# The 640-point transform stages of a spectral filter, from quarter folds with a remainder chunk to five 128x128 tables by residues modulo 5

## The chip, the core and the metric

The kernel runs on one core of a Trainium2 chip. The metric is the device time of one execution in microseconds (us), the median over the runs shown. TensorE multiplies, VectorE and ScalarE read the results out of PSUM and do the elementwise work, GpSimd makes tables and SyncE (SP) issues nearly all DMAs; each engine works through its own queue in the order in which the program gives it instructions.

## What is computed

The reference, cut to what matters: a layer norm, a global spectral filter over the 2048 x 640 tile, a gated feed-forward network on the same normalised input, and a sum.

```python
xn = _layernorm(x)                                  # x: 1 x 2048 x 640, bf16
X  = rfft2(xn.astype(float32))                      # over (2048, 640): 2048 x 321
s  = irfft2(X * (w_r + 1j * w_i), s=(2048, 640)).astype(bfloat16)
g  = silu((gelu(xn @ w_gate) * (xn @ w_up)) @ w_down)   # 640 -> 1536 -> 640
out = x + s * g
```

## The kernel before, in words

Row n = 16 n2 + n1 of x is partition n2 of slab n1: 16 slabs of 128 x 640. The 2048-point transform is split into 16 x 128 and the 640-point transform uses the symmetry of cosine and sine. The stages of the spectral part are, slab by slab:

- **fold** (`fold_a`, `fold_b` with `fold4`, two slabs at a time, VectorE): sums and differences of a row with its mirror image, so that a 640-long row becomes five chunks of 128 columns. Four chunks are full quarters, the fifth collects the remaining columns.
- **S1** (`slab_S1`): five matmuls of a chunk by the 128-point table `Tfwd`, 128 columns each; ScalarE casts the result to Z.
- **D** (`slab_D` with `d_matmuls`, L481 to 484): the 640-point stage. Four outputs of 161 columns, and for each one matmul by `FT` and one by the remainder table `TR`: eight matmuls of 161 columns. ScalarE casts it to `zd`, a DMA writes it to DRAM (`ZDR`).
- **load_B2**, then 16 **quads** (`quad_S2`, `quad_S2i`): the 16-point stage on 64x64 quarters of TensorE (`px`), a cast to `xs` by ScalarE, two products with the filter tables W1 and W2 on VectorE (`p1`, `p2`), the inverse 16-point stage (`pu`), a cast, and DMAs to DRAM (`UDR`).
- **load_V**, **vfold** (VectorE, as the fold), **S1i** (five matmuls of 128 columns) and **Di** (`slab_Di`, again `d_matmuls`): ScalarE scales the result to `eo`, VectorE makes the two halves of a row of Y from it by one addition and one subtraction (L587, L588).
- **finish / multiply_add** (L596 to 598): Y times the gate G plus x, and the DMA of a row to the output.

The feed-forward network is what TensorE mostly does: for each group g of four slabs twelve tiles t of the gate (`psg`) and of the up projection (`psu`), five matmuls each (L623); ScalarE makes `ge` from psg (L628), VectorE multiplies it with psu to uT (L630); then the down projection (L647), `th` (ScalarE, L677) and G (VectorE, L678). psg and psu have two PSUM banks each, all results of the spectral stages share two further buffers (`psB`).

The order is written out by hand. The list `back` holds the network in 144 **slots**: slots 0 to 13 are 256 columns of a tile (both projections), slots 14 to 23 half a tile each (512 columns of psg in even slots, of psu in odd ones), slots 24 to 35 the down projection of group 0 in thirds; then 24 half tiles and 12 thirds for each further group: 36 to 71, 72 to 107, 108 to 143. `plan[s]` lists what of the spectral part follows in slot s, and every engine gets its instructions in that order. So an instruction that waits holds up all that stand behind it on its engine. Before, S1 and D of slab 4 onward stand some three slots apart up to slot 58, the quads at 66 to 91, S1i and Di at 102 to 134. The sine tables of the second half of the 128-point table are made by ScalarE in slot 22 (`tinv_sin`, `mg_sin`; two loads of the activation table), the statistics and the norm (`stats`, `root4`, `norm`, `norm_act`) group by group ahead of the folds.

Of the kernel before, what the change touches and what calls it, by code (L numbers as in the profile page):

```python
# [14 lines left out]
P = 128  # L15
S = 2048
D = 640
# [13 lines left out]
def kernel(  # L31
# [36 lines left out]
    W1 = [wts.tile([P, 2, 8, L], BF16, name=f"W1{b}") for b in range(2)]  # L68
    W2 = [wts.tile([P, 2, 8, L], BF16, name=f"W2{b}") for b in range(2)]
# [6 lines left out]
def build(nc, env):  # L76
    consts, big, wts, xg, work, psA, psB = (env[k] for k in ("consts", "big", "wts", "xg", "work", "psA", "psB"))
# [26 lines left out]
    def w_rows(i, b, half, ri, pm):  # L104
        q0 = half * 64 + ri * 2 + pm
        return spw[i][0][b][q0:q0 + 61:4]

    def w_plus(i, b, half, ri):
        r = b * 16 + half * 8
        src = spw[i][1][:, 0:64].rearrange("k (a r) l -> k a r l", a=2)  # L110
        nc.sync.dma_start(out=w_rows(i, b, half, ri, 0), in_=src[:, :, r:r + 8, :])

    def w_minus(i, b, lo, half):
        sp = spw[i][1]
        WT = w_rows(i, b, half, 0, 1)
        r = 128 - lo * 32 - b * 16 - half * 8
        s0 = 1 if r == 128 else 0
        nc.sync.dma_start(out=WT[:, lo, s0:8, :], in_=sp[:, r - s0:r - 8:-1, :])
        if s0:
            nc.sync.dma_start(out=WT[:, lo, 0, :], in_=sp[:, 64, :])  # L120

    def w_dup(i, b, half):
        nc.sync.dma_start(out=w_rows(i, b, half, 1, 1), in_=w_rows(i, b, half, 0, 1))

    def w_edge(i, b):
        WT = spw[i][0][b].rearrange("p a s l -> p (a s) l")[:, :, 0:L:320]
        nc.gpsimd.tensor_scalar(out=WT, in0=WT, scalar1=0.5, scalar2=None, op0=ALU.mult)
# [3 lines left out]
    FT = consts.tile([P, 5, LH], BF16)  # L131
    TR = consts.tile([P, 2, 2, LH], BF16)
# [36 lines left out]
    lint = gtile([LH], INT32)  # L169
    nc.gpsimd.iota(lint, pattern=[[1, LH]], base=0, channel_multiplier=0)  # L170
    vt = gtile([NS, P], INT32)

# [21 lines left out]
    u_f, hi_f, s_f, h_f, g_f, pf, lo_b = bits("pb", [(0, 63), (6, 1), (0, 31), (5, 1), (5, 3), (0, 127), (0, 1)])  # L194
    ph_t = affine("ph_t", hi_f, -1536.0, 1536.0)
    e96 = c1("e96")
    nc.vector.tensor_single_scalar(out=e96, in_=pf, scalar=96.0, op=ALU.is_equal)
    a_m = affine("a_m", pf, 2.0, 64.0)
    b_o = affine("b_o", pf, 1.0, 32.0)
    sp_f = c1("sp_f")  # L200
    nc.vector.tensor_scalar(out=sp_f, in0=e96, scalar1=160.0, scalar2=s_f, op0=ALU.mult, op1=ALU.add)
    b_e = affine("b_e", h_f, -160.0, 160.0)
    a_r = affine("a_r", sp_f, 2.0, 0.0)
    b_r = c1("b_r")
    nc.vector.tensor_scalar(out=b_r, in0=sp_f, scalar1=hi_f, scalar2=b_e, op0=ALU.mult, op1=ALU.add)
# [39 lines left out]
    fv = gtile([3, LH], FP32)  # L245
    ftm = gtile([3, LH], FP32)

    def ft_angle():
        nc.scalar.activation(out=fv[:, 0], in_=lint, func=ACT.Identity, scale=a_m)
        nc.scalar.activation(out=fv[:, 1], in_=lint, func=ACT.Identity, scale=a_m, bias=b_o)  # L250
        nc.scalar.activation(out=fv[:, 2], in_=lint, func=ACT.Identity, scale=a_r, bias=b_r)
        nc.scalar.activation(out=ftm, in_=fv, func=ACT.Identity, scale=1.0 / 640.0, bias=magic)
        nc.scalar.activation(out=ftm, in_=ftm, func=ACT.Identity, bias=nmagic)

    def ft_wrap():
        nc.vector.scalar_tensor_tensor(out=fv, in0=ftm, scalar=-640.0, in1=fv, op0=ALU.mult, op1=ALU.add)

    def ft_sin():
        w = TWO_PI / 640.0 * (1.0 - 2e-7)
        nc.scalar.activation(out=ftm[:, 0:2], in_=fv[:, 0:2], func=ACT.Abs)  # L260
        nc.scalar.activation(out=FT[:, 1:4:2], in_=fv[:, 0:2], func=ACT.Sin, scale=w)
        nc.scalar.activation(out=FT[:, 4], in_=fv[:, 2], func=ACT.Sin, scale=w)
        nc.scalar.activation(out=FT[:, 0:4:2], in_=ftm[:, 0:2], func=ACT.Sin, scale=-w, bias=halfpi)

    def ft_rest():
        nc.gpsimd.memset(mhalf, -0.5)
        mk4 = consts.tile([P, 4], FP32)
        for g in range(4):
            nc.vector.tensor_single_scalar(out=mk4[:, g:g + 1], in_=g_f, scalar=float(g), op=ALU.is_equal)
        for g in range(4):  # L270
            nc.vector.tensor_scalar(out=TR[:, g // 2, g % 2, :], in0=FT[:, 4, :], scalar1=mk4[:, g:g + 1],
                                    scalar2=None, op0=ALU.mult)
        nc.gpsimd.memset(TR[32:33, 0, 0, 0:LH:2], 1.0)
        nc.gpsimd.memset(TR[32:33, 0, 0, 1:LH:2], -1.0)
# [144 lines left out]
    def fold4(dst, src, plus, minus):  # L419
        s4 = src.rearrange("p k (t d) -> p k t d", t=2)  # L420
        dm = dst[:, :, 0:512].rearrange("p k (g d) -> p k g d", g=4)
        dr = dst[:, :, 512:640].rearrange("p k (g d) -> p k g d", g=4)
        for gs, op in ((plus, ALU.add), (minus, ALU.subtract)):
            nc.vector.tensor_tensor(out=dm[:, :, gs, :], in0=s4[:, :, :, 32:160], in1=s4[:, :, :, 288:160:-1], op=op)
            nc.vector.tensor_tensor(out=dr[:, :, gs, 1:32], in0=s4[:, :, :, 1:32], in1=s4[:, :, :, 319:288:-1], op=op)

    def fold_a(pair):
        xn = X[:, 2 * pair:2 * pair + 2, :]
        assert ("n", 2 * pair + 1) in done
        uvt = work.tile([P, 2, D], BF16, tag="uv", bufs=1)  # L430
        nc.vector.tensor_tensor(out=uvt[:, :, 0:320], in0=xn[:, :, 0:320], in1=xn[:, :, 320:640], op=ALU.add)
        nc.vector.tensor_tensor(out=uvt[:, :, 320:640], in0=xn[:, :, 0:320], in1=xn[:, :, 320:640], op=ALU.subtract)
        xf[pair] = uvt

    def fold_b(pair):
        uvt = xf[pair]
        f = work.tile([P, 2, D], BF16, tag="xf", bufs=2)
        fold4(f, uvt, slice(0, 4, 3), slice(1, 3))
        nc.vector.tensor_copy(out=f[:, :, 512:D:32], in_=uvt[:, :, 0:D:160])
        xf[pair] = f  # L440
        done.add(("f", pair))

    def chunk(f, k, c):
        return f[:, k, c * P:(c + 1) * P]
# [25 lines left out]
    def slab_S1(n1):  # L470
# [3 lines left out]
        for c in range(5):  # L474
            nc.tensor.matmul(pz[:, c, :], lhsT=chunk(f, n1 % 2, c), rhs=Tfwd[:, n1, :], start=True, stop=True)  # L475
# [3 lines left out]
    def d_matmuls(ps, lhs):  # L479
        for b in range(2):  # L480
            for k in range(2):  # L481
                o = ps[:, b, k * LH:(k + 1) * LH]
                nc.tensor.matmul(o, lhsT=lhs[:, 2 * b + k, :], rhs=FT[:, 2 * b + k, :], start=True, stop=False)  # L483
                nc.tensor.matmul(o, lhsT=lhs[:, 4, :], rhs=TR[:, b, k, :], start=False, stop=True)  # L484

    def natural(ps):
        return ps[:, :, 0:LP].rearrange("p b (c m) -> p c m b", c=2)

    def slab_D(n1):
        pd = psB.tile([P, 2, 512], FP32, tag="b")  # L490
        d_matmuls(pd, Zt.pop(n1))
        zd = work.tile([P, 2, LP], BF16, tag="m2", bufs=3)
        nc.scalar.copy(out=zd.rearrange("p c (m b) -> p c m b", b=2), in_=natural(pd))  # L493
        nc.sync.dma_start(out=ZDR[:, n1].rearrange("c p l -> p c l"), in_=zd[:, :, 0:L])
# [12 lines left out]
    def quad_S2(j):  # L507
# [8 lines left out]
        nc.scalar.copy(out=xs, in_=px[:, :, 0:L])  # L516
        p1 = work.tile([P, 2, L], BF16, tag="p1", bufs=3)
        p2 = work.tile([P, 2, L], BF16, tag="p2", bufs=3)
        for pp, WT in ((p1, W1), (p2, W2)):
            nc.vector.tensor_tensor(out=pp, in0=xs, in1=WT[j // 8][:, :, j % 8, :], op=ALU.mult)  # L520
# [4 lines left out]
    def quad_S2i(j):  # L525
# [9 lines left out]
        us = work.tile([P, 2, L], BF16, tag="m2", bufs=3)  # L535
        nc.scalar.copy(out=us, in_=pu[:, :, 0:L])  # L536
        for lo in range(2):
            to = uv[lo][:, j // 8, :, j % 8, :]
            nc.sync.dma_start(out=to[:, :, 0:L], in_=us[lo * 64:lo * 64 + 32, :, :])
            nc.sync.dma_start(out=to[:, :, L:D], in_=us[lo * 64 + 32:lo * 64 + 64, :, 1:320])  # L540
# [12 lines left out]
    def vfold(pair):  # L553
        V = st_c["V"][:, 2 * pair:2 * pair + 2, :]
        f = work.tile([P, 2, D], BF16, tag="xf", bufs=2)
        fold4(f, V, slice(0, 4, 3), slice(2, 0, -1))
        nc.vector.tensor_tensor(out=f[:, :, 512:513], in0=V[:, :, 0:1], in1=V[:, :, 320:321], op=ALU.add)
        nc.vector.tensor_tensor(out=f[:, :, 576:577], in0=V[:, :, 0:1], in1=V[:, :, 320:321], op=ALU.subtract)
        nc.vector.tensor_copy(out=f[:, :, 544:D:64], in_=V[:, :, 160:D:320])
        st_c[("f", pair)] = f  # L560

# [157 lines left out]
    for n1 in range(4, NS):  # L719
        if n1 == 7:  # L720
            s += 2
# [138 lines left out]
```

## Time and profile before

| | |
|---|---|
| median of 3 runs | 211.51 us (211.3 to 211.68) |
| the profiled execution | 212.3 us, of which the span in the trace 210.5 us |
| busy time | TensorE 200.3 us, VectorE 138.2, ScalarE 127.7, GpSimd 19.2 |
| first and last matmul of the network | begins at 10.67 us, ends at 207.25 us |
| last instruction of VectorE | ends at 208.13 us |
| VectorE busy from 156.8 to 192.8 us | 31.31 of 36.00 us |

A row of the groups gives line, engine, operation, result and inputs, shape and count, then the busy time in us and the mean duration in ns of one, then the idle time of the engine before them and who ended it. In the timeline the first number is the start, the second the duration; independent instructions of one engine overlap a little, so the distance from start to start is below the duration. The chain of work is the path followed back from the last instruction; in order of time its rows give start, length and what ran.

### The profile page before, as it was taken

The page shows a single profiled execution, that of the slowest core. Times are in us where ns is not written, and L with a number is a line of the kernel's source. Part 1 is how long each engine was busy: PE and PEld are TensorE (multiplying, and loading weights), DVE is VectorE, ACT ScalarE, POOL GpSimd, SP SyncE. Part 2 cuts the span into 40 slices and gives each one's busy share as a digit, 9 for nine tenths or more (in the row PEclk, how much of TensorE's full clock was granted, in tenths as well). Part 3 has the DMA queues.
Part 4 walks back from the last instruction along what each step waited for, and adds up shares of the span by engine and source line. Part 5 has one row for each costly group of instructions (what it writes and reads, how often), then busy time and mean ns, then how long its engine had stood idle before and what let it go on. Part 6 is the DMA issues. An engine that isn't in the chain of part 4 may idle for free.

```text
span 210.5 us, 4486 instructions
## 1 busy us (share of the span) xinstructions
PE 200.3 (95%) x1600; PEld 125.5 (60%) x1600; DVE 138.2 (66%) x436; ACT 127.7 (61%) x215; POOL 19.2 (9%) x53
## 2 busy tenths in 40 slices
PE   0699999999999999999999999999999999999993
PEld 0389984567765555666644434347776556666773
DVE  8878977975975662252566755423769888994443
ACT  7656567599575666532677767732466665665721
POOL 8000128720004000000000000000000000000000
PEclk9999999999999999999999999999999999999999
DMA  5999955765946575739963232328913443332221
GB/s 159 337 361 366 361 159 137 159 165 147 175 78 164 134 175 124 195 120 205 221 131 82 64 86 67 88 68 247 340 42 96 121 120 101 97 93 65 63 78 47
DMA packets 37222, 31.79 MB, mean 151 GB/s; under 512 B 11344, under 2 KB 35024, under 8 KB 37072
## 3 DMA queue, kind: packets, MB, share of 16 engines
q1 hardware_dynamic: 37200, 31.51, 55.5%
q8 instruction: 12, 0.20, 0.4%
q14 instruction: 10, 0.08, 0.1%
HBM read 20.34 MB, written 7.87 MB: 134 GB/s over the span
## 4 chain that ended last, share of the span: by engine, by line
PE 95%; DVE 3%; ACT 1%; issue 0%; POOL 0%; POOLq 0%
PE psg L623 25%; PE psu L623 25%; PE psg L647 13%; PE psu L647 12%; PE pu L533 2%; PE pz L475 2%; PE py L484 2%; PE pd L484 2%; PE pd L483 2%; PE py L483 2%; PE pv L572 2%; PE px L513 2%; PE pw L279 1%; DVE st L371 1%; ACT Tinv L219 1%; PE pt L453 1%
## 5 line engine op out<-in xcount | busy, mean ns | idle before, releaser
L623 PE MATMUL psg<-xnT,Wg 128*128 128x512 bf16 (+1 forms) x275 | 61.5, 355 | 0.0
L623 PE MATMUL psu<-xnT,Wu 128*128 128x512 bf16 (+1 forms) x275 | 61.2, 354 | 0.0
L630 DVE TENSOR_TENSOR uT<-psu,ge 128x512 bf16<-128x512 f32 (+1 forms) x55 | 34.0, 618 | 26.3 <-PE psu L623 25.0
L647 PEld LDWEIGHTS <-uT 128*128 128x128 bf16 x396 | 37.2, 98 | 14.3 <-issue 0.5
L628 ACT ACTIVATE ge<-psg 128x512 bf16<-128x512 f32 (+1 forms) x55 | 30.0, 546 | 20.4 <-PE psg L623 18.9
L623 PEld LDWEIGHTS <-Wg 128*128 128x128 bf16 x275 | 25.6, 99 | 20.0 <-issue 2.3
L623 PEld LDWEIGHTS <-Wu 128*128 128x128 bf16 x275 | 25.6, 99 | 19.7 <-issue 1.8
L647 PE MATMUL psg<-Wd,uT 128*128 128x320 bf16 (+1 forms) x204 | 31.1, 295 | 0.0
L647 PE MATMUL psu<-Wd,uT 128*128 128x320 bf16 (+1 forms) x192 | 28.9, 295 | 0.0
L520 DVE TENSOR_TENSOR p<-xs,W 128x642 bf16<-128x642 bf16 x32 | 14.5, 493 | 9.7 <-ACT xs L516 9.4
L584 ACT ACTIVATE eo<-py 128x644 bf16<-128x644 f32 x16 | 11.3, 707 | 9.8 <-PE py L484 9.6
L516 ACT CAST xs<-px 128x642 bf16<-128x642 f32 x16 | 11.1, 694 | 9.2 <-PE px L513 5.8
L493 ACT CAST zd<-pd 128x644 bf16<-128x644 f32 x16 | 11.1, 694 | 6.0 <-PE pd L484 6.0
L371 DVE BATCH_NORM_STATS2 st<-X 128x6 f32<-128x320 bf16 x32 | 13.9, 477 | 0.0
L596 DVE TENSOR_TENSOR Yall<-Yall,G 128x640 bf16<-128x640 bf16 (+2 forms) x21 | 8.7, 412 | 7.7 <-ACT G L683 7.3
L477 ACT CAST Z<-pz 128x640 bf16<-128x640 f32 x16 | 11.0, 688 | 4.0 <-PE pz L475 4.0
L574 ACT CAST vs<-pv 128x640 bf16<-128x640 f32 x16 | 11.0, 688 | 2.0 <-PE pv L572 2.0
L536 ACT CAST us<-pu 128x642 bf16<-128x642 f32 x16 | 11.2, 700 | 0.9 <-PE pu L533 0.9
L678 DVE SCALAR_TENSOR_TENSOR G<-th,psg 128x320 bf16<-128x320 f32 x12 | 5.8, 482 | 8.8 <-ACT th L677 8.7
L677 ACT ACTIVATE th<-psu 128x320 f32<-128x320 f32 x12 | 5.3, 439 | 8.6 <-PE psu L647 8.5
L483 PE MATMUL py<-FT,vs 128*128 128x161 bf16 x64 | 10.5, 233 | 0.0
L483 PE MATMUL pd<-FT,Z 128*128 128x161 bf16 x64 | 10.5, 233 | 0.0
(140 smaller groups left out, 235.8 us busy)
## 6 DMA issues: line engine op xcount, KB each, us to landing
ZDR<-zd SPq DMA_DIRECT2D x16, 160.5 KB, 3.0
B<-ZDR SPq DMA_DIRECT2D x8, 321.0 KB, 7.2
xt<-in_A_x_dram SPq DMA_DIRECT2D x16, 160.0 KB, 2.4
Wg<-in_B_w_gate_dram SPq DMA_DIRECT2D x4, 480.0 KB, 7.4
Wu<-in_B_w_up_dram SPq DMA_DIRECT2D x4, 480.0 KB, 8.4
X<-in_A_x_dram SPq DMA_DIRECT2D x3, 640.0 KB, 9.1
Wd<-in_B_w_down_dram SPq DMA_DIRECT2D x1, 1920.0 KB, 13.9
Vin<-UDR SPq DMA_DIRECT2D x3, 640.0 KB, 7.6
```

What stands on the lines that cost most here:

```text
L371: nc.vector.bn_stats(out=st[:, k, :], in_=xr[:, k, :])
L477: nc.scalar.copy(out=Zt[n1], in_=pz)
L483: nc.tensor.matmul(o, lhsT=lhs[:, 2 * b + k, :], rhs=FT[:, 2 * b + k, :], start=True, stop=False)
L493: nc.scalar.copy(out=zd.rearrange("p c (m b) -> p c m b", b=2), in_=natural(pd))
L516: nc.scalar.copy(out=xs, in_=px[:, :, 0:L])
L520: nc.vector.tensor_tensor(out=pp, in0=xs, in1=WT[j // 8][:, :, j % 8, :], op=ALU.mult)
L536: nc.scalar.copy(out=us, in_=pu[:, :, 0:L])
L584: nc.scalar.activation(out=eo.rearrange("p c (m b) -> p c m b", b=2), in_=natural(py), func=ACT.Copy, scale=(2.0 if n1 >= 12 else 1.0) / ( ...
L623: nc.tensor.matmul(ps, lhsT=WT[:, c, t * P:(t + 1) * P], rhs=xnT[g][:, c, c0:c1_], start=(c == 0), stop=(c == 4))
L628: late.append(lambda: nc.scalar.activation(out=ge, in_=ps, func=ACT.Gelu_apprx_tanh))
L630: nc.vector.tensor_tensor(out=uT[g][:, t, c0:c1_], in0=ps, in1=cur["ge"], op=ALU.mult)
L647: nc.tensor.matmul(ph, lhsT=uT[g][:, t, j * P:(j + 1) * P], rhs=Wd[:, t, c0:c1_], start=(t == 0), stop=(t == NT - 1))
```

## The change

- **Fold.** `fold_a` adds and subtracts a slab and its mirror image in pieces of 64 columns to T (two additions of 640 columns per pair of slabs). `fold_b` makes two differences of 512 columns and two scaled additions (`scalar_tensor_tensor`, 512 columns each, factors 0.618 and -1.618), `fold_c` three additions of 512, 256 and 256. They stand in three slots of their own for each pair.
- **D** is five matmuls of 128 columns by blocks of a new table FT (640 columns); TR and its making go. `zd` is written into one of three buffers `ZB`.
- **Di** is five matmuls of 128 columns by FI, five transposes of FT (`fi_turn`, slot 61). **vfold goes**: the inverse quads write their rows to DRAM in the order that S1i needs, with two casts on ScalarE and one on VectorE (256 columns each) in place of one of 642 on ScalarE. In its place stand `spread_a` and `spread_b` after Di, per pair of slabs: two scaled additions, four additions of 512 columns and two of 640; L587 and L588 go.
- `multiply_add` of slabs 0 to 11 stands at slots written out (109 to 139) and no longer where its inputs are ready; the rows of x that it adds are loaded into W1 once the filter is used up.
- **Filter loads**: one tile each for W1 and W2, 28 DMAs in place of 48, in slots 14 to 47; edges in slot 55.
- **Order.** The pairs' folds, S1 and D stand at slots written out, the second sine tables are made in slot 26 in place of 22, the statistics, roots and norms are moved, D ends in slot 56, quads stand at 65 to 89 with the inverse part ahead of the forward one, S1i and Di at 98 to 130.

The core of the diff (after.py against before.py):

```diff
-    def fold_b(pair):
-        uvt = xf[pair]
-        f = work.tile([P, 2, D], BF16, tag="xf", bufs=2)
-        fold4(f, uvt, slice(0, 4, 3), slice(1, 3))
-        nc.vector.tensor_copy(out=f[:, :, 512:D:32], in_=uvt[:, :, 0:D:160])
+    def fold_b(pair):
+        W = xf[pair].rearrange("p a k (m d) -> p (a k) m d", d=64)
+        NM = work.tile([P, 2, 4, 2, 64], BF16, tag="nm", bufs=1, name="NM")
+        nm = NM.rearrange("p i q x d -> p q i x d")
+        for x, i0, i1 in ((0, slice(4, 2, -1), slice(1, 3)), (1, slice(0, 2), slice(3, 1, -1))):
+            nc.vector.tensor_tensor(out=nm[:, :, :, x, :], in0=W[:, :, i0, :], in1=W[:, :, i1, :], op=ALU.subtract)
+        f = work.tile([P, 5, 2, P], BF16, tag="xf", bufs=2, name="f")
+        fc = f[:, 1:5].rearrange("p (a c) k d -> p c a (k d)", c=2)
+        for c, g in ((0, TAU), (1, -NU)):
+            nc.vector.scalar_tensor_tensor(out=fc[:, c], in0=NM[:, 1].rearrange("p (a k) x d -> p a (k x d)", a=2), scalar=g,
+                                           in1=NM[:, 0].rearrange("p (a k) x d -> p a (k x d)", a=2),
+                                           op0=ALU.mult, op1=ALU.add)
+    def fold_c(pair):
+        T, f = xf[pair]
+        W = T.rearrange("p a k (m d) -> p (a k) m d", d=64)
+        pq = work.tile([P, 4, 2, 64], BF16, tag="pq", bufs=1, name="pq")
+        nc.vector.tensor_tensor(out=pq, in0=W[:, :, 1:3, :], in1=W[:, :, 4:2:-1, :], op=ALU.add)
+        nc.vector.tensor_tensor(out=pq[:, :, 0, :], in0=pq[:, :, 0, :], in1=pq[:, :, 1, :], op=ALU.add)
+        nc.vector.tensor_tensor(out=f[:, 0].rearrange("p k (a d) -> p a k d", a=2),
+                                in0=pq[:, :, 0, :].rearrange("p (a k) d -> p a k d", a=2),
+                                in1=T[:, :, :, 0:64], op=ALU.add)
...
     def slab_D(n1):
-        d_matmuls(pd, Zt.pop(n1))
+        for c in range(5):
+            nc.tensor.matmul(pair_of(cols, *FWD[c]), lhsT=Z[:, c, :], rhs=block2(FTf, c), start=True, stop=True)
...
+        us = ZB[j % 3].rearrange("p (h r q) -> p h r q", h=2, r=6)
+        nc.scalar.copy(out=us[:, :, 1:4:2, :], in_=residues(pu, 1, 1))
+        nc.scalar.copy(out=us[:, :, 2:5:2, :], in_=residues(pu, 4, -1))
+        nc.vector.tensor_copy(out=us[:, :, 0:6:5, :], in_=residues(pu, 0, 5))
...
+    def spread_a(pair):
+        nc.vector.scalar_tensor_tensor(out=NM[:, 0].rearrange("p q x d -> p q (x d)"), in0=H, scalar=TAU, in1=G,
+                                       op0=ALU.mult, op1=ALU.add)
+        nc.vector.scalar_tensor_tensor(out=NM[:, 1].rearrange("p q x d -> p q (x d)"), in0=G, scalar=TAU, in1=H,
+                                       op0=ALU.mult, op1=ALU.subtract)
+        nc.vector.tensor_tensor(out=Eb[:, :, 4:2:-1, :], in0=a2, in1=nm[:, :, :, 0, :], op=ALU.add)
+        nc.vector.tensor_tensor(out=Eb[:, :, 1:3, :], in0=a2, in1=nm[:, :, :, 0, :], op=ALU.subtract)
+    def spread_b(pair):
+        nc.vector.tensor_tensor(out=Eb[:, :, 0:2, :], in0=Eb[:, :, 0:2, :], in1=m12, op=ALU.add)
+        nc.vector.tensor_tensor(out=Eb[:, :, 3:1:-1, :], in0=Eb[:, :, 3:1:-1, :], in1=m12, op=ALU.subtract)
+        nc.vector.tensor_tensor(out=up, in0=e4[:, 0], in1=e4[:, 1], op=ALU.add)
+        nc.vector.tensor_tensor(out=down, in0=e4[:, 0], in1=e4[:, 1], op=ALU.subtract)
...
+    fold_at = ((3, 5, 7), (8, 10, 12), (19, 20, 22), (26, 28, 30), (32, 33, 35), (38, 41, 43), (45, 46, 48), (49, 50, 52))
+    s1_at = ((9, 10, 11, 12), (14, 15, 16, 17), (23, 24, 26, 27), (31, 32, 34, 35), (36, 38, 39, 41), (44, 45, 47, 48),
+             (49, 50, 51, 52), (53, 54, 55, 56))
+    for g, st, nf in ((1, (13, 14, 15, 16), (18, 20)), (2, (23, 24, 26, 27), (31, 33)), (3, (36, 37, 39, 40), (44, 46))):
...
-    put(19, tinv_wrap, 1)
-    put(22, tinv_sin, 1)
-    put(22, mg_sin)
+    put(21, tinv_wrap, 1)
+    put(26, tinv_sin, 1)
+    put(26, mg_sin)
+    put(z_end + 1, mg_build)
+    put(z_end + 3, mg_turn)
+    put(z_end + 5, fi_turn)
...
+    for p in range(8):
+        sd = vs0 + 4 * p + 5 if p < 7 else s
+        put(sd + 1, spread_a, p)
+        put(sd + 2, spread_b, p)
+    for n1, sl in enumerate((109, 114, 119, 124, 129, 131, 133, 134, 135, 136, 138, 139)):
+        put(sl, multiply_add, n1, 0, D)
```

In `s1_at` the four numbers of a pair are the slots of S1 and S1, D and D of its two slabs; in `fold_at` the three are the slots of `fold_a`, `fold_b`, `fold_c`; z_end is 56, vs0 is 98.

## Prediction

> **What bounds it now.** I read the page's totals, the slices and the chain first.
>
> ```profile
> PE 200.3 (95%) x1600; PEld 125.5 (60%) x1600; DVE 138.2 (66%) x436; ACT 127.7 (61%) x215; POOL 19.2 (9%) x53
> ...
> DVE  8878977975975662252566755423769888994443
> ...
> PE 95%; DVE 3%; ACT 1%; issue 0%; POOL 0%; POOLq 0%
> ```
>
> TensorE is the chain; from 10.67 to 207.25 us it never waits for long. But VectorE, 66% on average, is at 7 to 9 tenths at both ends, where the folds and the inverse stage lie. So each matmul removed is worth its time only while VectorE and ScalarE keep up. The chain in order of time gives TensorE's prices:
>
> ```profile
> 6.88 1.86 PE pw L279 x4
> ...
> 70.81 0.28 PE pz L475 x5
> 71.09 1.08 PE psu L623 x5
> ...
> 72.73 1.08 PE psg L623 x5
> ```
>
> S1 (five matmuls of 128) takes 0.276, half a tile 1.08, and from 72.17 to 72.73 a D stage fits: 0.545 for eight matmuls of 161. VectorE's prices come from the groups (mean ns of one is the number behind busy) and its timeline:
>
> ```profile
> L424 DVE TENSOR_TENSOR f<-uvt 128x512 bf16<-128x512 bf16 x16 | 6.8, 424 | 0.1
> L431 DVE TENSOR_TENSOR uvt<-X 128x640 bf16<-128x640 bf16 x8 | 4.0, 494 | 4.1 <-ACT X L411 3.6
> L256 DVE SCALAR_TENSOR_TENSOR GEN<-GEN 128x483 f32<-128x483 f32 x1 | 0.7, 657 | 0.0
> ```
>
> ```profile
> 164.47 0.49 DVE L596 TENSOR_TENSOR Yall<-Yall,G 128x640 bf16<-128x640 bf16 x1
> 165.00 0.49 DVE L597 TENSOR_TENSOR Yall<-Yall,xt 128x640 bf16<-128x640 bf16 x1
> 165.41 0.68 DVE L630 TENSOR_TENSOR uT<-psu,ge 128x512 bf16<-128x512 f32 x1
> ```
>
> An instruction that needs the one before it starts 0.04 after its end (164.47 to 165.00), any other 0.08 before it (165.00 to 165.41).
>
> **TensorE.** 32 stages (16 D, 16 Di) fall from 0.545 to the 0.276 of five matmuls of 128: -8.6. The five transposes of `fi_turn` add 0.28. Together **-8.3**.
>
> **VectorE, per pair of slabs.** Additions of n bf16 columns: 0.49 for 640, 0.42 for 512, 0.29 for 256 (between the 124 and 320 column rows, 0.22 and 0.33). That 64-column runs and reversed blocks cost no more I take from L424, which reads backwards in two dimensions. A scaled addition of 512 bf16 columns isn't in the trace: from below 0.42 (the addition), from above 0.69 (L256, 483 columns in 0.657, a column per tick). I take 0.69, the same operation. [...]
>
> With the distances: fold_a 0.82; fold_b 0.34 + 0.46 + 2 x 0.61 = 2.03; fold_c 0.46 + 0.33 + 0.21 = 1.00. So 3.85 where the old fold took 1.83 (17.34 to 19.50 less a uT). Spread_a 0.61 + 0.73 + 0.34 + 0.46 = 2.15, spread_b 0.34 + 0.46 + 0.82 = 1.63: 3.78 where vfold (1.22) and four additions of L587, L588 (1.1) took 2.3. The casts of `us` add about 0.34 (256 columns out of PSUM; the 0.42 of a uT of 256) in the quads, where VectorE is at 5 to 7 tenths. VectorE's total rises by some 34 us to 172, against 192 of TensorE: no spare at the ends.
>
> **Waits ahead of S1.** TensorE takes S1 in order, so if fold_c is late everything waits. For each pair I add up both queues from a common point. In slots: uT 0.61, stats 1.04, norm 0.4, G 0.41; TensorE 1.08 per half tile, 1.09 per third, 0.276 per unit; uT starts 0.12 after its matmuls.
>
> - *Slot 23.* From the end of slot 18: VectorE stands behind the uT of slot 19 until 1.2, then uT 0.61, fold_a 0.82, fold_b 2.03, norm 0.4, uT 0.61, the wrap of the angles 0.6, fold_c 1.08: 7.35. TensorE arrives after five half tiles, 5.42. **Wait 1.9.**
> - *Slot 31.* ScalarE holds the second sine tables now in slot 26, one slot pair ahead of a fold:
>
> ```profile
> 43.01 1.28 ACT L219 ACT_TABLE_LOAD   x1
> 44.31 1.15 ACT L219 ACTIVATE Tinv<-GEN,negpi 128x1024 bf16<-128x1024 int32 x1
> ...
> 45.84 0.67 ACT L477 CAST Z<-pz 128x640 bf16<-128x640 f32 x1
> 46.53 1.28 ACT L677 ACT_TABLE_LOAD   x1
> 47.82 0.44 ACT L677 ACTIVATE th<-psg 128x320 f32<-128x320 f32 x1
> ```
>
> ```profile
> 48.29 0.49 DVE L678 SCALAR_TENSOR_TENSOR G<-th,psg 128x320 bf16<-128x320 f32 x1 [2.29 <-ACT th L677]
> ```
>
>  From the load to the end of `th` it is 5.25, and already VectorE stood 2.29 for it; nothing hung on that then. Now the G of slot 28 stands ahead of fold_b. From the end of slot 26: zd 0.8, the block 5.27, then G 0.41, fold_b 2.03, G 0.41, fold_c 1.08: 10.05. TensorE: 1.36 + 1.09 + 1.54 + 1.09 + 1.09 = 6.17. **Wait 3.9.**
> - *Slots 36, 44, 49*, each from the S1 where both met: 7.6 against 6.5; 11.0 against 9.8; 7.0 against 6.5. **Waits 1.1, 1.2, 0.5.** The first two pairs and the last come in time.
> - *Slot 59*: mg_build (1.54 in the trace, 89.19 to 90.73) has one slot less ahead of mg_turn: 0.2.
>
> Together **+8.8**. Nothing of it is hidden: the matmuls behind S1 are in the same queue.
>
> **The inverse end.** From the start of slot 104 VectorE waits 2.2 for a G, then has to the uT of slot 131 seven spreads (26.5), twelve uT (7.3), five multiply-adds (0.53 + 0.41 each, 4.7), two G (0.8): 41.5, TensorE 37.8. The twelfth matmul of the down projection would want that uT 1.0 after: **wait 2.8**. Behind that uT are spread_a and spread_b of the last pair (3.8), seven multiply-adds (6.6) and nine pieces of the last group (5.2): 15.5, TensorE ends 12.1 after it; VectorE ends 3.4 after TensorE where it now ends 0.9 after. **+2.4.**
>
> **Cost at nothing.** The filter loads are fewer and early; `w_dup` blocks SP, where its partners landed some slots before. B2 has 9 slots from the last D (8 before, when its first DMA landed 4.3 after issue and nobody waited). V: its first part landed at about 144.7, S1i began at 149.25; the three slots fewer leave 1 to 2 us. If that cover is gone S1i waits up to 1. The new order of pu and px leaves their 0.63 per quad. ScalarE's two casts of 256 for one of 642 add 0.08 a quad, beside an engine with room. GpSimd's early root is off the path: the norm behind it stands behind slot 19's uT anyway. At the start VectorE saves 1 us of tables, but the second slab's statistics wait for x; at most -0.2, not counted.
>
> **Sum.** -8.3 + 8.8 + 2.8 + 2.4 = +5.7. The profiled execution would be 212.3 + 5.7 = 218.0, the median, 0.8 below it, **217.2 us**.
>
> **Rivals.**
>
> 1. *The scaled addition takes 0.42.* The waits shrink to 6.6, the tail to 2.1: +0.4, 211.9, no slower within the measurement (about 0.2% can be told apart). This is the case from the other side; it decides at about 0.41 us per instruction, and every row of this operation speaks against it. 0.11.
> 2. *The front is covered*: fold_c ready before TensorE comes to S1 in all five places, because VectorE's queue is shorter than my sums by 0.5 to 4 us. Then -8.3 + 0.2 + 5.2, 208.6. For it: before, the one fold that was late cost 0.2 (the trace has f L424 once as the releaser of S1). Against: 2 us more per pair. 0.12.
> 3. *VectorE keeps up everywhere*: 211.5 - 8.3 = 203.2; needs 16 us of new folds for nothing. 0.06.
> 4. *TensorE slows down after the long wait.* After its first idle stretch the four matmuls of 512 took 1.86, 0.465 each, where five now take 1.08. Repeated after slot 31, some 3.5 us at half rate: +1.8, 219.0. [...] My wait of 3.9 is hardly longer, so 0.10.
> 5. *Runs of 64 columns go at a column per tick*: 512 columns in 0.69, 640 in 0.82. 1.7 more per pair and stage; twelve pairs on the path, +20, 238. L424 speaks against it. 0.06.
>
> The forecast keeps 0.55. **Range** 207.1 to 221.4: it takes in rivals 1, 2 and 4 and an error of 0.3 us per step, down from rival 2 by five late folds (1.5), up from rival 4 by eight spreads (2.4); 3 and 5 and the edges are left out. **Chances**: faster 2, 3 and a third of 1, 0.21; the same 0.04; slower 0.75.
>
> **What would show it.** TensorE idle ahead of `pz` five times, the longest in the first third of down projections behind the sine block; `pd` and `py` at 0.28; VectorE at 9 tenths in the last 50 us and its end 3 us after TensorE's; `NM<-E` at 0.69. Wrong if `NM` rows show 0.42, if `pz` doesn't wait for f, or if the last G waits for TensorE as now.

## The result and the profile after

The changed kernel took **218.68 us** (218.42 to 219.25, three runs) against 211.51: ratio 1.034, 95% interval 1.031 to 1.038. The profiled execution took 218.68 us, 6.4 more than the one before (212.3), its span is 216.9. From the page: the busy time of each engine, two rows of the slices (the span in 40 equal parts, a digit for the busy or granted tenths of each), the engines' shares of the chain.

```profile
PE 194.7 (90%) x1509; PEld 117.3 (54%) x1509; DVE 165.2 (76%) x429; ACT 126.9 (59%) x231; POOL 20.7 (10%) x56
...
DVE  6888898975677979734477777843249999999994
...
PEclk9999999999679999999999999999999999999999
...
PE 61%; DVE 27%; issue 6%; ACT 3%; DMA 1%; DVEq 0%
```

Matmuls went, and TensorE is 90% busy in place of 95%; VectorE has 27% of the chain in place of 3% and is at nine tenths from slice 31 on. One thing is new: in slices 11 and 12 the clock granted to TensorE (PEclk) is down to 6 and 7 tenths. Two rows of the waits of TensorE (us in total, times, longest):

```profile
PE pz L504 <- DVE f L469: 8.2, 5, 3.8
...
PE psg L699 <- DVE uT L682: 0.8, 1, 0.8
```

S1 waits five times for the last addition of a fold. How the longest comes about is in the chain of work, in order of time:

```profile
47.79 1.28 ACT L220
49.08 1.15 ACT Tinv L220
...
51.30 1.28 ACT L729
52.60 0.45 ACT th L729
...
53.07 0.49 DVE G L730
53.55 0.68 DVE NM L454 x2
...
54.26 1.29 DVE f L458 x2
...
56.65 0.30 DVE f L469
```

ScalarE loads the sine table, makes Tinv, loads the table back, makes `th`; G waits for that, the fold (NM, f) stands behind G, and S1 of slot 31 behind the fold. TensorE's timeline goes on from there (in brackets its idle time):

```profile
57.00 0.71 PE L504 MATMUL pz<-Tfwd,f 128*128 128x128 bf16 x5 [3.85 <-DVE f L469]
57.50 2.34 PE L699 MATMUL psu<-Wd,uT 128*128 128x320 bf16 x8
59.64 0.74 PE L504 MATMUL pz<-Tfwd,f 128*128 128x128 bf16 x5
60.17 3.00 PE L699 MATMUL psg<-Wd,uT 128*128 128x320 bf16 x12
63.00 0.71 PE L699 MATMUL psu<-Wd,uT 128*128 128x320 bf16 x4
```

Behind the wait eight matmuls of 320 take 2.14 from start to start (57.50 to 59.64) where they take 1.09 elsewhere: half rate. Over the first four pieces it costs 0.22 + 1.05 + 0.25 + 1.20 = 2.7 us, so it lasts twice that, some 5.5 us.

**Where the 6.4 us are.** The uT of slot 131, TensorE's last run of matmuls and VectorE's last instruction, first before (without the uT), then after:

```profile
206.25 0.99 PE L647 MATMUL psg<-Wd,uT 128*128 128x160 bf16 x12
...
207.89 0.24 DVE L597 TENSOR_TENSOR Yall<-Yall,xt 128x160 bf16<-128x160 bf16 x1
```

```profile
198.47 0.68 DVE L682 TENSOR_TENSOR uT<-psu,ge 128x512 bf16<-128x512 f32 x1
...
209.97 0.99 PE L699 MATMUL psg<-Wd,uT 128*128 128x160 bf16 x12
...
214.04 0.24 DVE L653 TENSOR_TENSOR Yall<-Yall,W 128x160 bf16<-128x160 bf16 x1
```

TensorE's last run begins at 209.97 in place of 206.25: +3.7. Counted from start to start of its matmuls, that is

- +0.3: the first matmul of the network begins at 10.93, before at 10.67;
- -0.6: its first two pieces take 0.78 and 0.55, before 1.06 and 0.85 (0.55 is full rate);
- -8.7: shorter stages D and Di, less the transposes of `fi_turn`;
- +9.0: the five waits, each some 0.16 more than its idle time, since the profile draws a matmul's end 0.16 behind the start of the next one (`pd` at 25.90 ends at 26.34, the next begins at 26.18);
- +2.7: half rate;
- +0.3: `mg_turn` of slot 59, whose four transposes take 0.50 in place of 0.22 because VectorE's tables MG and MJ come late;
- +0.9: the last group's wait;
- -0.2: two small waits that the kernel before had.

VectorE ends 4.3 after that start (214.28) and ended 1.9 after it before (208.13): +2.4. The last 0.2 lie behind VectorE's end.

### The profile page after: what moved, and what is told of

The parts are those of the page before. It is cut to its first block, busy times and chain, and to the rows that moved or that the text cites. A ratio compares the mean times of both kernels' runs of the same rounds, so it can differ in the third digit from the quotient of the medians.

```text
span 216.9 us, 4312 instructions
## 1 busy us (share of the span) xinstructions
PE 194.7 (90%) x1509; PEld 117.3 (54%) x1509; DVE 165.2 (76%) x429; ACT 126.9 (59%) x231; POOL 20.7 (10%) x56
## 4 chain that ended last, share of the span: by engine, by line
PE 61%; DVE 27%; issue 6%; ACT 3%; DMA 1%; DVEq 0%
PE psu L675 16%; PE psg L675 15%; PE psu L699 9%; PE psg L699 9%; DVE uT L682 5%; DVE Yall L652 3%; PE pu L563 3%; PE pz L504 3%; DVE Yall L653 2%; DVE NM L625 2%; DVE NM L623 2%; DVE f L458 2%; PE pd L514 2%; DVE NM L454 1%; DVE Yall L643 1%
## 5 line engine op out<-in xcount | busy, mean ns | idle before, releaser
L699 PEld LDWEIGHTS <-uT 128*128 128x128 bf16 x396 | 37.8, 100 | 16.0 <-DVE uT L682 1.1
L675 PEld LDWEIGHTS <-Wg 128*128 128x128 bf16 x275 | 25.3, 98 | 19.8 <-issue 2.3
L699 PE MATMUL psg<-Wd,uT 128*128 128x320 bf16 (+1 forms) x204 | 32.1, 303 | 0.8 <-DVE uT L682 0.8
L699 PE MATMUL psu<-Wd,uT 128*128 128x320 bf16 (+1 forms) x192 | 30.3, 302 | 0.0
L504 PE MATMUL pz<-Tfwd,f 128*128 128x128 bf16 x80 | 7.7, 231 | 8.2 <-DVE f L469 8.2
L614 ACT ACTIVATE E<-py 128x640 bf16<-128x640 f32 x16 | 11.3, 703 | 5.9 <-PE py L611 5.9
L730 DVE SCALAR_TENSOR_TENSOR G<-th,psu 128x320 bf16<-128x320 f32 x12 | 5.8, 486 | 10.9 <-ACT th L729 10.9
L516 ACT CAST zu<-pd 128x640 bf16<-128x640 f32 x16 | 11.0, 689 | 3.9 <-PE pd L514 3.9
L504 PEld LDWEIGHTS <-f 128*128 128x128 bf16 x80 | 5.8, 103 | 12.5 <-DVE f L469 10.5
L566 ACT CAST zu<-pu 128x256 bf16<-128x256 f32 x16 | 6.0, 372 | 9.4 <-PE pu L563 5.5
L568 DVE CAST zu<-pu 128x256 bf16<-128x256 f32 x16 | 6.8, 423 | 5.7 <-ACT zu L567 5.7
```

Of the source, the lines that this page charges most:

```text
L504: nc.tensor.matmul(pz[:, c, :], lhsT=f[:, c, n1 % 2, :], rhs=Tfwd[:, n1, :], start=True, stop=True)
L516: nc.scalar.copy(out=zd[:, 1:2 * LP - 1].rearrange("p (c l) -> p c l", c=2)[:, :, 0:320] .rearrange("p c (q r) -> p c q r", r=5), in_=flat ...
L614: nc.scalar.activation(out=st_c["E"][:, n1 % 2, :], in_=flat, func=ACT.Copy, scale=(2.0 if n1 >= 12 else 1.0) / (S * D))
L675: nc.tensor.matmul(ps, lhsT=WT[:, c, t * P:(t + 1) * P], rhs=xnT[g][:, c, c0:c1_], start=(c == 0), stop=(c == 4))
L699: nc.tensor.matmul(ph, lhsT=uT[g][:, t, j * P:(j + 1) * P], rhs=Wd[:, t, c0:c1_], start=(t == 0), stop=(t == NT - 1))
L730: nc.vector.scalar_tensor_tensor(out=G, in0=th, scalar=1.0, in1=ph, op0=ALU.add, op1=ALU.mult)
```

## Experiments

Times are medians. The kernel before was measured beside each group of experiments, at 211.9 to 212.1 us. The changed kernel was not measured again, so differences to its 218.68 are uncertain by some 0.5 us.

**filled: does the idle time cause the half rate?**

```diff
+    put(31, warm_up, 16)
     for sl, it in f_units.items():
         put(sl, *it)
```

> The changed kernel with sixteen more matmuls of 512 columns, whose result nobody reads, ahead of S1 in slot 31: they fill 3.5 of the 3.85 us for which TensorE stands there, and shorten no wait of another engine. Theory (TensorE drops to half rate because it idled): the 6.5 us behind the wait pass at full rate, 2.7 us less, 216.0 us. Rival (the slow stretch comes from what else runs then, DMA, the sine block, or from the work itself): 218.7 or more, since the matmuls can only add.

216.51 us (215.91 to 218.44). TensorE's timeline of filled:

```profile
52.69 3.62 PE L296 MATMUL pw<-Tinv,ident 128*128 128x512 bf16 x16
56.69 0.45 PE L504 MATMUL pz<-Tfwd,f 128*128 128x128 bf16 x5 [0.39 <-DVE f L469]
56.98 1.25 PE L699 MATMUL psu<-Wd,uT 128*128 128x320 bf16 x8
```

S1 comes no sooner than in the changed kernel (56.69 against 57.00; this execution was 0.3 ahead already at the S1 of slot 23), and the eight matmuls behind it have full rate. Sixteen useless matmuls make the kernel 2.2 us faster (the profiled execution 2.8): the half rate is the price of the idling. Shown. One of the four executions, without a trace, took 218.44 us; TensorE was granted 0.986 of the full clock on average (0.994 in the traced one); it seems to have had a slow stretch elsewhere.

**filled4: how long an idle time is enough?** `put(31, warm_up, 4)` in place of 16.

> The changed kernel with four unread matmuls of 512 columns (0.87 us) ahead of S1 in slot 31 in place of the sixteen of filled: TensorE's longest wait is then about 3.0 us, between those of 2.1 that no slow stretch followed and the one of 3.3 (plain_adds) that one followed. If an idle time of 3.0 is enough for half rate: 218.7. If not: 216.0, as filled.

217.29 and 216.2 us. The profiled execution, the slower one, waited 2.98 us, and half rate followed for 1.7 us of cost. Over all traces: waits of up to 2.1 us inside the network had none behind them; 2.98, 3.31, 3.52, 3.85 and 4.87 had it, at a cost of 1.7 to 2.7. By the granted clock the half rate lasts 3.41 us behind the three shorter of these waits and 6.83 us behind the longer ones. It need not begin with the work: in the changed kernel it runs from 55.78 to 62.61, so 1.2 us of it fall into the wait, and in filled4 from 57.85 to 61.26, 1.2 us behind the end of the wait.

Executions without a trace show that the line is not sharp. One of the ten of plain_adds (whose traced wait is 3.31) took 212.03 us at a mean granted clock of 0.994, the other nine 213.52 to 215.02 at 0.981 to 0.987: it seems to have escaped. Two of the four of sine_early, where no wait in the trace is over 2.1, had granted clocks of 0.985 and 0.986 (below).

**sine22: the sine block moved back, with what feeds it.**

```diff
-    put(17, tinv_angle, 1)
-    put(17, mg_phase)
-    put(21, tinv_wrap, 1)
-    put(25, mg_wrap)
-    put(26, tinv_sin, 1)
-    put(26, mg_sin)
+    put(12, tinv_angle, 1)
+    put(14, mg_phase)
+    put(19, tinv_wrap, 1)
+    put(20, mg_wrap)
+    put(22, tinv_sin, 1)
+    put(22, mg_sin)
```

> The changed kernel with one part undone: the second sine tables are made in slot 22 again, ahead of the first down projections, and GpSimd's and VectorE's steps that feed them stand where they stood (slots 12 to 20). Theory (ScalarE's 5.2 us block in slot 26 holds the G in front of fold_b, and so S1 of slot 31): the wait of 3.85 us falls to about 1.5, what VectorE itself is late, TensorE never idles for over 3 us in the body and the half-rate stretch behind it (2.7 us) goes: 218.7 - 2.3 - 2.7 = 213.7 us. If the slow stretch has nothing to do with the wait, it stays: 216.4. Rival, VectorE's longer folds alone make that wait: nothing changes, 218.7.

218.91 us, a miss by 5.2. The wait of slot 31 fell from 3.85 to 1.21 as expected, but slot 23 now waited 4.87 and had a half-rate stretch of its own. VectorE's timeline of sine22 names the cause:

```profile
39.30 0.45 DVE L432 TENSOR_SCALAR X<-X,mva,nrn 128x640 bf16<-128x640 bf16 x1 [3.69 <-POOL nrn L420]
```

On GpSimd the phases (`mg_phase`) now stood ahead of the root of the second group; the norm waited for the root, and the fold behind it. The changed kernel has the root first (nrn at 34.44, the phases from 37.19 on); I had undone two things at once.

**sine_early: the same, with GpSimd's steps in slot 4.**

> The changed kernel with the second sine tables in slot 22 again, and GpSimd's steps that feed them (the angles and the phases, 9 us together) in slot 4, where GpSimd has nothing to do until the statistics of the second group are there; so the root of that group is not held up, as it was in the run sine22 (it came 3.7 us later there and S1 of slot 23 waited 4.87 us). Theory (two causes had been mixed there: the sine block in front of the fold of slot 28, and the root behind the phases): the wait of slot 23 is about 2.0 again, that of slot 31 about 1.2 as in sine22, no wait over 3, no slow stretch: 218.7 - 2.6 - 2.7 = 213.4 us. Rival (a shorter wait at one place comes back at the next, VectorE's total in front decides): 218.7.

216.87 us, 1.8 faster than the changed kernel, 3.5 slower than expected. In the traced execution (216.18 us) the waits are as expected (2.08 in slot 23, 1.44 in slot 31) and there is no half rate, but TensorE has a new wait:

```profile
28.18 0.44 PE L514 MATMUL pd<-FT,Z 128*128 128x128 bf16 x5 [1.92 <-POOL FT L267]
```

GpSimd's memset of FT now stood behind the phases: again its queue, and 1.9 us of the miss. Two of the four executions took 217.56 and 217.98 us at mean granted clocks of 0.985 and 0.986, the other two 216.18 at 0.995. That is the size of one stretch of half rate (3.4 us, 1.7 us of cost); no trace shows where.

**late_S1: fold and S1 where VectorE and TensorE have room.**

```diff
-(19, 20, 22), (26, 28, 30)
+(19, 20, 24), (26, 28, 30)
...
-(23, 24, 26, 27), (31, 32, 34, 35), (36, 38, 39, 41), (44, 45, 47, 48),
+(26, 27, 28, 29), (33, 34, 35, 36), (38, 39, 40, 42), (45, 46, 47, 48),
```

> As sine_early, and fold_c of the third pair in slot 24 in place of 22 (behind the last uT of group 0, where VectorE has only the G to make), and S1 and D of pairs 3 to 7 of the eight some one to three slots later. Theory (TensorE has other matmuls for these slots; a late fold costs only as much as S1 comes too early): the five waits, 5.9 us in sum by the rows so far, fall to about 1.8 (0.7 for the last uT ahead of the first down projection, 1.1 ahead of S1): 213.4 - 4.1 = 209.3 us. Rival (the end is bound by VectorE's total, so what TensorE gains in front it loses at the end): 213.4.

211.29 us, 5.6 less than sine_early (4.1 expected). The forecast of 209.3 was missed by 2.0, because it started from sine_early's forecast and so lacked the 1.9 for FT, which are still there. S1 waits 0.6 in sum, and all ten executions have a granted clock of 0.992 to 0.996. VectorE ends as before 4.3 behind the start of TensorE's last run (206.19 against 201.91). So the time gained on the waits in front is not lost again at the end: shown.

**plain_adds: VectorE's price taken away.** `scalar_tensor_tensor(...)` becomes `tensor_tensor(..., op=ALU.add)`, or subtract for the one that subtracts.

> The changed kernel with each of the 32 scaled additions of 512 columns on VectorE (two a fold, two a spread) replaced by a plain addition or subtraction of the same operands, so the factors 0.618 and 1.618 are left out of the computation. VectorE's rows fall from 0.69 to 0.42, 0.54 per pair and stage. Theory (VectorE's length sets the waits in front and the whole end): the waits ahead of S1 fall by about 2.4 in sum, that of slot 31 to 3.3, the wait ahead of the last down projections goes (0.8), and the end, where VectorE works without a gap for 53 us, falls by its 16 instructions, 4.3: 218.7 - 2.4 - 4.3, about 212.0, and some 2 less if the wait is then too short for the slow stretch. Rival (TensorE with its waits on other engines sets the end): only the front's 2.4, 216.3.

214.2 us (212.03 to 215.02, ten runs): 4.5 less, 6.7 to 8.7 expected. In front nearly as forecast: waits 6.2 in place of 8.2, and still half rate (a cost of 1.7 behind the wait of 3.31). The last group's 0.8 went too. But VectorE's 4.3 in the end did not come in full: its end lies 3.7 behind the start of TensorE's last run (209.96 against 206.28), where it was 4.3.

**long_D: TensorE gets its time back.**

```diff
             nc.tensor.matmul(pair_of(cols, *FWD[c]), lhsT=Z[:, c, :], rhs=block2(FTf, c), start=True, stop=True)
+        for c in range(5):
+            nc.tensor.matmul(flat[:, 768:896], lhsT=Z[:, c, :], rhs=block2(FTf, c), start=True, stop=True)
```

(and the same in `slab_Di`)

> The changed kernel with five more matmuls of 128 columns, to unused columns, behind each of the 32 stages D and Di, which makes them as long as before (0.55 us): TensorE gets its 8.6 us back and no other engine's work changes. Theory (the time saved on TensorE was spent waiting for VectorE wherever VectorE is late): in front some 1.8 of the 4.3 are taken out of waits, at the end VectorE sets the time and TensorE may take 4.1 more before it does: +3.6 in all, 222.3 us. Rival (the saving counts in full): +8.6, 227.3. Rival (VectorE sets the time everywhere): 218.7.

223.89 us: 5.2 more, where 3.6 were expected (the added matmuls take 8.9 from start to start). Both misses (plain_adds and this one) have one cause, my reading of the end as one stretch of VectorE work. It is two. Until the uT of slot 131 VectorE is only 0.8 late, so TensorE takes 0.8 and not 4.1 before it counts; what stands behind that uT (15.1 us) can't be done earlier in a queue that keeps its order, however idle VectorE becomes ahead of it. With that long_D comes to 1.8 in front (4.3, less 1.5 of waits and 1.0 of half rate) + 3.5 (16 Di, 4.3, less 0.8) = 5.3.

**cast_end: VectorE relieved at the end.**

```diff
+            if g == 3:
+                up = work.tile([P, 512], BF16, tag="up", bufs=2, name="up")
+                nc.scalar.copy(out=up, in_=ps)
+                ps = up
             nc.vector.tensor_tensor(out=uT[g][:, t, c0:c1_], in0=ps, in1=cur["ge"], op=ALU.mult)
...
-    for n1, sl in enumerate((109, 114, 119, 124, 129, 131, 133, 134, 135, 136, 138, 139)):
+    for n1, sl in enumerate((109, 113, 117, 121, 125, 129, 131, 133, 134, 135, 136, 138)):
```

> The changed kernel, only its last group different: ScalarE casts psu to bf16 (512 columns, about 0.6 us) and VectorE multiplies two bf16 operands (0.42 in place of 0.69), which takes 3.2 us off VectorE in the stretch where it never idles and puts 7 us on ScalarE; one multiply-add more stands ahead of slot 131. Theory (up to the uT of slot 131 VectorE is only 0.8 late, what it has to do behind that uT, 15.1 us against 11.8 of TensorE, is the rest): the 0.8 go, and 0.9 for the multiply-add: 217.0. Rival (every microsecond of VectorE in the stretch without gaps counts): 214.6. Rival (ScalarE becomes late): 218.7 or more.

216.17 us, 2.5 less (1.7 expected; 0.3 of the difference is an earlier start in the profiled run). The last group waits no more, and VectorE ends 3.3 behind the start of TensorE's last run where it was 4.3: the one multiply-add that now stands ahead. Of the 3.2 us taken from VectorE ahead of slot 131 only the 0.8 show.

**late_S1_cast: both.**

> late_S1 and cast_end together. Theory (front and end are two separate accounts): 209.3 - 1.7 = 207.6 us, faster than the kernel before by 1.8%. Rival (the end is one account with the front): 211.7 or more.

209.39 us, 1.9 under late_S1 (1.7 expected): the two accounts add up. The 1.8 above the forecast of 207.6 are again the wait for FT. Ratio to before 0.988 (0.985 to 0.991).

**best: GpSimd's steps in slot 7, behind its memsets.**

> late_S1_cast with GpSimd's angles and phases in slot 7 in place of 4, behind its two memsets in FT and those of the borders: there they had stood ahead of FT's last memset, and the first D waited 1.92 us for it. Theory: that wait goes and nothing else changes: 209.4 - 1.9 = 207.5 us, 2% under the kernel before. Rival (the D behind it was late by something else too): 209.4.

**207.01 us** (206.71 to 207.25), ratio 0.975 (0.973 to 0.978): faster than both kernels and 2.4 less than late_S1_cast (1.9 expected). TensorE's waits in best, behind its first:

```profile
PE pz L504 <- ACT X L428: 0.4, 1, 0.4
...
PE pz L504 <- DVE f L469: 0.2, 1, 0.2
PE psg L703 <- DVE uT L686: 0.2, 1, 0.2
```

**best_long_D: what the shorter stages are worth now.**

> best with five more matmuls of 128 columns, to unused columns, behind each D and Di, as in long_D. Theory (in best VectorE hardly holds up TensorE any more, so that TensorE's shorter stages count nearly in full): of 8.6 us about 0.8 vanish in what waits are left and in the fixed end: 207.5 + 7.8 = 215.3. In the changed kernel the same addition cost 5.2 (223.9 against 218.7). Rival (VectorE's total still decides): +5 as there, 212.5.

214.75 us, 7.7 more, where the same addition cost 5.2 in the changed kernel. With VectorE in time the shorter D and Di are worth 7.7 of the 8.9 that the added matmuls take.

**best_pool: part of the end on GpSimd.**

```diff
-        nc.vector.tensor_tensor(out=Y, in0=Y, in1=xts[n1][:, c0:c1_], op=ALU.add)
+        add = nc.gpsimd if 7 <= n1 < 12 else nc.vector
+        add.tensor_tensor(out=Y, in0=Y, in1=xts[n1][:, c0:c1_], op=ALU.add)
```

> best with the second addition of five multiply-adds (slabs 7 to 11, behind the uT of slot 131, 640 bf16 columns each) on GpSimd in place of VectorE. No row shows such an addition on GpSimd; estimate from its row L210 (1024 int32 columns in 1.2 us): 0.8 to 1.5 us each. Theory (VectorE's work behind that uT, some 14 us against TensorE's 11.8, sets the end): 2.05 us less on VectorE, which then ends about 0.9 behind TensorE: 207.5 - 1.6 = 205.9. Rival (GpSimd and VectorE get in each other's way): VectorE's rows beside GpSimd grow by as much, 207.5 or more.

209.88 us, 2.9 slower than best: the rival came true. GpSimd's timeline (first fence) and VectorE's (second) of best_pool:

```profile
199.62 1.41 POOL L654 TENSOR_TENSOR Yall<-Yall,W 128x640 bf16<-128x640 bf16 x1 [0.67 <-DVE Yall L652]
```

```profile
199.81 1.40 DVE L654 TENSOR_TENSOR Yall<-Yall,W 128x320 bf16<-128x320 bf16 x1
```

An addition of 320 columns takes VectorE 0.33 us alone and 1.40 here: it ends (201.21) only after GpSimd's (201.03), which had begun before it (199.62 before 199.81). The same holds for one VectorE instruction beside each of GpSimd's five additions; by VectorE's groups of best_pool and best these five together lose 5.6 us where 2.05 were to be saved. Why VectorE is held up no run shows.

## Why the prediction was right, and where it was off

- **TensorE, -8.3.** Right but for a little: a stage takes 0.28 (`pd` at 25.90, the next matmul at 26.18). The old one took 0.56 from start to start and not 0.545 (`py` at 186.06, the next at 186.62), so it is -8.7.
- **VectorE's prices.** Right: the scaled additions take 0.69 (groups of the changed kernel, below), so rival 1 falls, and 512 columns in runs of 64 take 0.42, so rival 5 does. It is these rows that show it: L424 reads backwards along one dimension only, in runs of 128. What the prediction calls a column per tick is 1.05 ns a column in the rows of the kernel before (uT of 256 columns in 0.417 us, of 512 in 0.686). VectorE's total, 172 forecast, came to 165.2; no term of the sum hangs on it.

```profile
L458 DVE SCALAR_TENSOR_TENSOR f<-NM 128x512 bf16<-128x512 bf16 x16 | 10.3, 688 | 0.3
...
L454 DVE TENSOR_TENSOR NM<-T 128x512 bf16<-128x512 bf16 x16 | 6.1, 423 | 0.1
```

- **Waits ahead of S1, +8.6 without mg_turn.** 1.9, 3.9, 1.1, 1.2, 0.5 forecast for slots 23, 31, 36, 44, 49; measured 2.01, 3.85, 0.68, 1.07, 0.61, together 8.2 of idle time; the 0.2 of `mg_turn` came as 0.3. sine_early shows the sine block as the cause of most of the longest, late_S1 that all of them are a matter of place. Rivals 2 and 3 fall.
- **"TensorE slows down after the long wait", rival 4.** I kept it out of the sum, at 0.10. It came, and cost 2.7 and not 1.8: the half rate lasted 5.5 us, not 3.5. In the sum this is the step that failed. The first wait of the trace (6.9 us, then four matmuls at 0.465) had hinted at it, though it lies at the start, where TensorE had done nothing yet. No row of the kernel before shows the 3.5 us, or how long TensorE has to idle for it, so the 0.10 rested on nothing measured. In the traces half rate followed idle times of 2.98 to 4.87 us, for 3.41 or 6.83 us: with a wait of 3.9 this should have been the likelier case.
- **"Wait 2.8" of the last group.** Mis-sized: 0.78. VectorE needed 40.2 from the start of slot 104 to that uT, not 41.5 (mainly the seven spreads: 25.3, not 26.5, since 3.78 holds the pauses between dependent instructions, and where a uT or a multiply-add stands inside, a spread adds only 3.6), and the eleven matmuls ahead of the twelfth took 1.66, not 1.0.
- **VectorE's end, +2.4.** Right: 15.1 us behind the uT of slot 131 (15.5 forecast), 3.3 after TensorE's end (3.4 forecast).
- **Start, "at most -0.2".** It became +0.3. In the chain VectorE's wrap of the angles (L215) takes 0.79 where it took 0.57; GpSimd's second table of indices is made beside it until 5.36, before only until 5.04. In all thirteen traces with the new order L215 ends at 5.91 or 5.92, whether it begins at 5.05 or at 5.16, so a wait for GpSimd would fit. No run moved the table.

So 5.7 were forecast and 6.4 came for the profiled execution (by the medians +7.2, 211.51 to 218.68; 217.2 had been forecast): +2.7 that I had left to a rival, -1.9 for the last group's wait, made too long, and small ones: -0.4 for the stages, +0.5 for the waits in front, +0.3 and -0.6 at the start, -0.2 for the small waits before and +0.2 behind VectorE's end. The near hit of the total is in part luck: its two largest errors have opposite signs.

## What to carry to other kernels

Matmuls saved by more elementwise work are worth their time only where the engine that does that work is in time at each place where TensorE asks for it: add up both queues from a common point, and then shift the asking (S1 some slots later) before giving up the change; here that, with the sine block and the folds put where ScalarE and VectorE have room and a little less work for VectorE at the end, turned +3.4% into -2.5%. The kernel before was not given the same care. That it has little to gain from it is argued and not tried: its network waits for nothing that the table of waits shows, and VectorE ends 0.9 us behind TensorE. What stands behind the last instruction that TensorE needs is an account of its own, and slack gained ahead of it does not help. And undoing a move means undoing it on every queue: two of the misses here came from GpSimd's order alone.

## What the runs showed of the hardware

- In the traces an idle TensorE of 2.98 to 4.87 us was followed by half rate, for 3.41 or 6.83 us by the granted clock, at a cost of 1.7 to 2.7 us; idle times up to 2.1 us inside the network cost only themselves. Single executions without a trace fit neither bound, by their granted clocks (plain_adds once at 0.994, sine_early twice, at 0.985 and 0.986).
- A bf16 addition of 640 columns took GpSimd 1.40 to 1.53 us in best_pool (VectorE 0.49), and a VectorE multiplication or addition of bf16 rows of Y that began beside it did not end before it: 0.2 to 0.35 us after it in five cases of five.
